# Transfers that take time by size in a planned schedule, merged first loads, copies moved to ScalarE, and later weights converted two at a time

## The chip, the cores and the metric

The kernel runs on one core of a Trainium2 chip. The metric is the device time of one execution in microseconds. Of the kernel before there are three timed executions and one that was profiled. Engines are named as in the profile: PE is TensorE (PEld its weight loads), DVE is VectorE, ACT is ScalarE, POOL is GpSimd, SP issues most transfers.

## The reference

Block-causal attention in float32 over 8 batches and 8 heads, 576 positions of 64 dimensions, and then a feed-forward layer on the 4608 tokens with a parametric ReLU:

```python
scores = (1 / sqrt(64)) * q @ k.T            # 8 x 8 x 576 x 576
mask = (pos[:, None] // 64) >= (pos[None, :] // 64)
attn = softmax(where(mask, scores, -1e9))    # sum + 1e-9 in the divisor
x = (attn @ v)                               # to (4608, 512)
h = x @ w_in                                 # 512 -> 2048
g = maximum(h, 0) + alpha * minimum(h, 0)
out = g @ w_out                              # 2048 -> 512
```

Two of the inputs, w_in and w_out, arrive as float64 (the kernel gets them as pairs of int32) and are turned into float32 on the chip.

## The kernel before

The whole program is a list of operations made by `op(engine, cost, fn, reads, writes, prio, ...)`. `Plan.schedule` (line 121) plays them through once with the costs given and fixes the order in which each engine gets its instructions; at each step an engine takes the ready operation of the lowest `prio` for which buffers are free. On the chip each engine then runs its instructions in exactly that order, and waits where an operand is not there yet. A transfer costs its queue a fixed time (450 to 3300 ns by place) and is over a fixed `LAT` later, whatever its size.

*Attention* runs over 32 pairs of heads, four pairs to a batch. `query_tile` computes a tile of 128 queries: scores on PE, row maximum on DVE (L786, L792), exponential on ACT (L795), sum and reciprocal on DVE (L799, L801), scaling on POOL (L803), transposes on PE (L812) and a copy to SBUF by `evac` (L889 on DVE, L891 on ACT in the first five pairs, NV = 5, which use plain float32). `values` multiplies by v. The first four pairs have their first 256 queries done ahead, from loads of their own (`early`, `load_q`), and pair 0 is done wholly in this way (`rest`). Later pairs are laid out by `prep`, with ten transfers from SBUF to SBUF per pair (L680).

*Weights* are converted by `to_f32` (L396): one transfer of 512 KB, four to five steps on DVE (L411, L416, L420, L425, L428), two on ACT (L414, L423), with two PSUM banks per conversion in flight. `split` (L431) then makes a high part on ACT and a low part on POOL. Six of sixteen slices f of the hidden layer are converted at the start (`first_weights`); the other ten after the attention (`later_weights`), in pairs, each as the factors of a seven-product scheme (`pair1`, L590), with priorities 1000 + f for w_in and 0.5 more for w_out.

*First phase* of the feed-forward layer (`chunk_a`, L512 and L549): 256 tokens at a time through the first six slices, filled in between the attention's work; partial sums go to memory. *Second phase*: 512 tokens at a time (`factors` loads xb and makes seven factors of x; L590 makes hidden parts, L549 multiplies by w_out into one accumulator for each 128 tokens), the other ten slices, and `store_out` adds the partial sums.

PSUM's eight banks are shared out by quotas: six for attention, one for hidden parts (`hp`), one accumulator (`acc`); when the attention ends, two for `hp`, four for `acc` and two for conversions (`words`, one conversion at a time). Some buffers of the second phase, four of the seven factors of x among them, exist only when the first phase has ended (`second_room`). When the last weight is converted, its two banks go to `hp`.

## Time and profile before

| | us |
|---|---|
| median of 3 runs | 1171.3 (1171.28 to 1174.82) |
| profiled execution | 1172.41 |
| its span, first to last instruction | 1170.6 |
| mean granted clock of TensorE | 0.99 |
| busy: PE, DVE, ACT, POOL | 1130.8, 846.4, 724.3, 598.6 |

The span is what the rows below are measured in; the profiled execution's own time lies 1.8 us above it. The engines' busy times add up to far more than the span, as they work side by side. A busy TensorE is not always a TensorE at full pace: products are pipelined, and one that waits for an operand or a bank can count as busy.

### The profile page before, as it was taken

Reading aid. Unit: us, or ns where it says so; the run is one execution under the profiler, and the core shown is the slowest. Engines: PE = TensorE matmul, PEld = TensorE weight load, DVE = VectorE, ACT = ScalarE, POOL = GpSimd, SP = SyncE. Lnnn points to the kernel's source line nnn. Section 1 sums busy time; section 2 is a strip of 40 time slices with the busy share of each in tenths; the row PEclk is TensorE's granted clock in tenths of the full one; section 3 lists DMA queues with packets and bytes.
Section 4 is the critical chain, followed back from the end, with each engine's and each line's share of the span. In section 5 each row is a group of like instructions: output and inputs, shape, how many; then the busy total and the mean of one; then the engine's idle time right before and its main releaser. Section 6 shows DMA issues by size and latency. Waiting matters only on the chain.

```text
span 1170.6 us, 22141 instructions
## 1 busy us (share of the span) xinstructions
PE 1130.8 (97%) x7345; PEld 1010.0 (86%) x7345; DVE 846.4 (72%) x1988; ACT 724.3 (62%) x1940; POOL 598.6 (51%) x771
## 2 busy tenths in 40 slices
PE   6999999999999999999999998999999999999997
PEld 3666899999999999899998986889989898989996
DVE  6988888888887877787867899756556564656543
ACT  5777888878778878687864766543434343343431
POOL 3655555656655556555445978642424344352431
PEclk8999999999999999999999999999999999999999
DMA  7897767776757666647404543302121121212021
GB/s 196 229 251 220 183 181 179 202 199 164 188 138 194 173 166 194 176 111 206 130 19 158 154 152 100 101 19 98 36 73 55 55 73 36 98 38 82 1 73 54
DMA packets 74098, 150.94 MB, mean 129 GB/s; under 512 B 9728, under 2 KB 11520, under 8 KB 73984
## 3 DMA queue, kind: packets, MB, share of 16 engines
q1 hardware_dynamic: 73120, 148.48, 45.2%
q8 instruction: 58, 0.95, 0.4%
q10 hardware_dynamic: 864, 1.06, 0.3%
q14 instruction: 56, 0.46, 0.1%
HBM read 66.33 MB, written 28.31 MB: 81 GB/s over the span
## 4 chain that ended last, share of the span: by engine, by line
PE 84%; DMA 5%; DVE 4%; ACT 2%; POOL 2%; issue 1%; SPq 1%; ACTq 0%; POOLq 0%; DVEq 0%
PE bank L549 32%; PE bank L590 18%; PE bank L512 11%; PE bank L927 6%; PE bank L812 5%; PE bank L779 5%; PE bank L843 2%; PE bank L917 1%; DMA K<-kraw 1%; DMA kraw<-in_k 1%; PE bank L871 1%; DMA Q<-qraw 1%; DMA qraw<-in_q 1%; ACT p L795 1%; SPq L680 1%
## 5 line engine op out<-in xcount | busy, mean ns | idle before, releaser
L532 POOL TENSOR_TENSOR gl<-g,gh 128x256 fp32r<-128x256 f32 x288 | 218.2, 766 | 317.2 <-PE bank L590 150.6
L590 PEld LDWEIGHTS bank<-X,w 128*128 128x128 f32 x1890 | 254.3, 190 | 24.1 <-POOL w L434 3.8
L590 PE MATMUL bank<-X,w 128*128 128x256 f32 x1890 | 260.5, 283 | 4.6 <-POOL w L434 3.4
L549 PE MATMUL bank<-w,gh 128*128 128x512 f32 x720 | 226.4, 395 | 3.0 <-ACT gh L529 2.1
L523 ACT ACTIVATE g<-bank 128x256 f32<-128x256 f32 x288 | 110.4, 385 | 184.5 <-DVE bank L603 164.2
L803 POOL TENSOR_SCALAR p<-p,ri 128x256 f32<-128x256 f32 (+3 forms) x256 | 142.9, 572 | 115.9 <-DVE ri L801 60.6
L529 ACT CAST gh<-g 128x256 fp32r<-128x256 f32 x288 | 117.1, 408 | 73.3 <-DVE g L525 71.8
L525 DVE SCALAR_TENSOR_TENSOR g<-g,oal,bank 128x256 f32<-128x256 f32 x288 | 135.4, 475 | 32.3 <-ACT g L523 28.2
L603 DVE TENSOR_TENSOR bank<-bank,g 128x256 f32<-128x256 f32 x180 | 75.6, 428 | 101.0 <-PE bank L590 78.5
L795 ACT ACTIVATE p<-bank,nm 128x256 f32<-128x256 f32 (+3 forms) x256 | 134.1, 532 | 23.0 <-DVE nm L792 14.3
L549 PE MATMUL bank<-w,gl 128*128 128x512 f32 x360 | 142.0, 395 | 0.3 <-POOL gl L532 0.2
L549 PE MATMUL bank<-wa,gh 128*128 128x512 f32 x432 | 140.6, 406 | 0.3 <-POOL wa L434 0.3
L549 PEld LDWEIGHTS bank<-w,gh 128*128 128x128 f32 x720 | 121.6, 189 | 17.2 <-ACT gh L529 2.5
L512 PE MATMUL bank<-xh,wa 128*128 128x256 f32 x864 | 132.3, 289 | 1.8 <-DVE xh L498 1.0
L894 DVE TENSOR_TENSOR PL<-bank,PH 128x512 fp32r<-128x512 f32 (+2 forms) x189 | 111.6, 608 | 16.8 <-ACT PH L893 13.9
L512 PEld LDWEIGHTS bank<-xh,wa 128*128 128x128 f32 x864 | 115.1, 190 | 5.9 <-DVE xh L498 1.6
L812 PE MATMUL bank<-ident,p 128*128 128x128 f32 x640 | 102.7, 279 | 10.7 <-POOL p L803 7.9
L779 PE MATMUL bank<-K,Q 128*128 128x512 f32 (+1 forms) x472 | 102.0, 333 | 0.9 <-DVE xT L948 0.4
L893 ACT CAST PH<-bank 128x512 fp32r<-128x512 f32 (+2 forms) x189 | 96.4, 529 | 10.5 <-PE bank L812 7.5
L599 DVE TENSOR_TENSOR g<-bank,g 128x256 f32<-128x256 f32 x135 | 57.0, 422 | 56.2 <-PE bank L590 55.1
L812 PEld LDWEIGHTS bank<-ident,p 128*128 128x128 f32 x640 | 73.7, 141 | 20.5 <-POOL p L803 11.7
L927 PE MATMUL bank<-PH,V 128*128 128x320 f32 x324 | 87.6, 286 | 2.0 <-DVE g L525 1.0
(130 smaller groups left out, 2070.7 us busy)
## 6 DMA issues: line engine op xcount, KB each, us to landing
Q<-QH SPq DMA_DIRECT2D x62, 288.0 KB, 4.4
K<-KH SPq DMA_DIRECT2D x124, 144.0 KB, 3.7
vraw<-in_v SPq DMA_DIRECT2D x32, 320.0 KB, 3.3
xd<-xT SPq DMA_DIRECT2D x8, 1152.0 KB, 5.9
part<-o SPq DMA_DIRECT2D x36, 256.0 KB, 3.6
xb<-xd SPq DMA_DIRECT2D x9, 1024.0 KB, 5.4
ob<-part SPq DMA_DIRECT2D x36, 256.0 KB, 2.7
out<-ob SPq DMA_DIRECT2D x36, 256.0 KB, 2.0
```

The costliest lines, as they stand in the source:

```text
L512: nc.tensor.matmul(hp()[:, :n], ww()[:, 0, cc * P:(cc + 1) * P], x()[:, cc, :n], start=(i == 0 and cc == 0), stop=(i == 2 and cc == NCC - 1))
L525: op("DVE", c_dve(CHA) + 60, lambda: nc.vector.scalar_tensor_tensor(out=g(), in0=g(), scalar=oal[:, f:f + 1], in1=hp()[:, ts], op0=ALU.mul ...
L529: op("ACT", c_act(CHA, True), lambda: nc.scalar.copy(out=gh(), in_=g()), r=[g], w=[gh], prio=FP)
L532: op("POOL", c_pool(CHA), lambda: nc.gpsimd.tensor_tensor(out=gl(), in0=g(), in1=gh().bitcast(F32), op=ALU.subtract), r=[g, gh], w=[gl], p ...
L549: nc.tensor.matmul(acc(), a()[:, ts], ww(), start=(first and i == 0), stop=(last and i == 2))
L590: nc.tensor.matmul(bank()[:, :CHA], W()[:, i, 256 * at + P * c:256 * at + P * c + P], B()[:, j, CHA * c:CHA * c + CHA], start=(n == 0), st ...
L779: nc.tensor.matmul(o, Q()[:, i, qs], K()[:, 2 * h + i, :w], start=(i == 0), stop=(i == 1))
L795: op("ACT", 238 + w / 1.2, lambda h=h, t=t: nc.scalar.activation(out=t()[:, :w], in_=sb[h]()[:, off[h]:off[h] + w], func=AF.Exp, bias=nm() ...
L803: op("POOL", 244 + w / 1.2, lambda h=h: nc.gpsimd.tensor_scalar(out=pts[h]()[:, :w], in0=pts[h]()[:, :w], scalar1=ri()[:, h:h + 1], scalar ...
L812: nc.tensor.transpose(out=tp()[:, base + c * P:base + (c + 1) * P], in_=pts[h]()[:, c * P:(c + 1) * P], identity=ident)
L894: op("DVE", c_dve(n) + (HALF if n == P else 0), lambda: nc.vector.tensor_tensor(out=lo(), in0=src(), in1=hi().bitcast(F32), op=ALU.subtrac ...
L927: nc.tensor.matmul(ob()[:, at + a - q0:at + q1 - q0], V()[:, c, 2 * h:2 * h + 2, :], t[:, h, 448 * c + a:448 * c + q1], start=(i == 0 and ...
```

## The change

What it does:

- The planner gives a transfer a time by its size in KB: 430 ns on the queue, 1300 ns to begin, 4.1 ns for each KB on one common pipe, 1000 ns to land, and no more than eight at once (the ninth waits on its queue). All transfers are now given by size.
- The first loads are merged: q of pair 0 in two transfers, q of pairs 1 to 3 in two, k of pairs 1 and 2 in one; they no longer wait for zeros. Zeros of pairs 1 to 3 go to POOL. k of pair 0 stays on ACT's queue; k of pair 3 and the first w_in move from ACT's queue to SP's, the latter with the priority E0 - 6.5. The buffers for these early q and k are others. Fixed parts of Q and K get priority 2 instead of 0.
- In the first five pairs, the second head's copies of tiles 2 and 3 go from DVE to ACT. The first step of a conversion writes the SBUF tile m instead of a PSUM bank, and ACT reads it from there.
- The first two of the later w_in are converted in the attention stage (priority 150, banks of the attention), the others two at a time (four banks for `words`). For that there are two accumulators at first; two banks go over from `words` to `acc` when the w_in of f = 12 is ready. The first xb gets priority 1006.7 instead of 0.

```diff
-BANKS, HB, AB, HT, AT, WB = 6, 1, 1, 2, 4, 2
+BANKS, HB, AB, HT, AM, AT, WB = 6, 1, 1, 2, 2, 4, 4
-XP = 0.0
+XP = 2.0
+SOON, XB = 150, 1006.7
+FEW = 12
-LAT = {"PE": 250, "DVE": 130, "ACT": 140, "POOL": 140, "SP": 3300, "ACTQ": 3000, "POOLQ": 3000}
+LAT = {"PE": 250, "DVE": 130, "ACT": 140, "POOL": 140}
+QUEUES = ("SP", "ACTQ", "POOLQ")
+ISSUE, BEGINS, LANDS, PER_KB, LANES = 430, 1300, 1000, 4.1, 8
...
+                if engine in QUEUES:
+                    begin = max([t, *lands[-LANES:][:len(lands) >= LANES]])
+                    end = begin + ISSUE
+                    pipe = max(begin + BEGINS, pipe) + cost * PER_KB
+                    lands.append(pipe + LANDS)
+                    lat = lands[-1] - end
...
-        op("DVE", c_dve(512), lambda: nc.vector.tensor_scalar(
-            out=e(), in0=high(), scalar1=0x7FF00000, scalar2=None, op0=ALU.bitwise_and),
-            r=[raw], w=[eb], claim=[fb, mb], prio=prio)
-        op("ACT", c_act(512), lambda: nc.scalar.activation(
-            out=e(), in_=e(), func=AF.Relu, bias=ebias, scale=8.0), w=[eb], prio=prio)
+        op("DVE", c_dve2(512), lambda: nc.vector.tensor_scalar(
+            out=mb().bitcast(I32), in0=high(), scalar1=0x7FF00000, scalar2=None, op0=ALU.bitwise_and),
+            r=[raw], w=[mb], claim=[fb, eb], prio=prio)
+        op("ACT", c_act(512, True), lambda: nc.scalar.activation(
+            out=e(), in_=mb().bitcast(I32), func=AF.Relu, bias=ebias, scale=8.0), r=[mb], w=[eb], prio=prio)
...
-                mb, w = to_f32(src[f].bitcast(I32), prio, queue="ACTQ" if f + i == 0 else "SP")
+                mb, w = to_f32(src[f].bitcast(I32), prio, early=E0 - 6.5 if f + i == 0 else None)
...
-            ms = [to_f32(w_in[f + i].bitcast(I32), prio(f), ["att"], "words") for i in range(2)]
+            ms = [to_f32(w_in[f + i].bitcast(I32), *((prio(f), ["att"], "words") if f > FA else (SOON, [], "att"))) for i in range(2)]
...
-        op("SP", 2900, lambda: nc.sync.dma_start(out=xb(), in_=xd[:, :, t0:t0 + CHB]),
-           ... w=[xb], prio=0)
+        op("SP", 1024, lambda: nc.sync.dma_start(out=xb(), in_=xd[:, :, t0:t0 + CHB]),
+           ... w=[xb], prio=0 if t0 else XB)
...
+    def early_loads():
+        def zeros(engine, ps):
+            for h in range(2):
+                rows = slice(64 - 64 * h, 128 - 64 * h)
+                engine.memset(xT[rows, ps, S + 256 * h:S + 256 * h + 256], 0.0)
+        pr = E0 - 8
+        op("DVE", 700, lambda: zeros(nc.vector, slice(0, 1)), w=[("zeros", 0)], prio=pr)
+        op("POOL", 1600, lambda: zeros(nc.gpsimd, slice(1, NP)), w=[("zeros", p) for p in range(1, NP)], prio=pr)
...
+        for p0, p1 in ((0, 1), (1, NP)):
+            for h in range(2):
+                hs = slice(64 * h, 64 * h + 64)
+                op("SP", 64 * (p1 - p0), lambda h=h, hs=hs, p0=p0, p1=p1: nc.sync.dma_start(
+                    out=xT[hs, p0:p1, S + 256 * h:S + 256 * h + 256],
+                    in_=qT[p0:p1, hs, 64 * h:64 * h + 256].rearrange("p r n -> r p n")), w=[("q", p, h) for p in range(p0, p1)], prio=pr)
+        for ps, to, queue in (((0,), lambda: o_k()[:, :256], "ACTQ"), ((1, 2), lambda: o_k2().rearrange("p (i n) -> p i n", i=2), "SP"),
+                              ((3,), lambda: KX[:, :256], "SP")):
+            issuer = {"SP": nc.sync, "ACTQ": nc.scalar}[queue]
+            op(queue, 128 * len(ps), ..., prio=pr + ps[0])
...
-                         p, "DVE" if j == 0 or j > 1 and h else "ACT", pr)
+                         p, "DVE" if j == 0 else "ACT", pr)
...
-        plan.quota["acc"] += AT - AB
+        plan.quota["acc"] += AM - AB
         plan.quota["words"] = WB
...
+    def more_sums():
+        plan.quota["acc"] += AT - AM
+        plan.quota["words"] -= AT - AM
+    op("NONE", 0, lambda: None, r=[(("w1", FEW, 6), "l")], prio=0, then=more_sums)
```

## Rows read from the trace of the kernel before

**Rows 1.** Busy time by stretch: length, then PE, PEld, DVE, ACT, POOL (instructions), clock, DMA share.

```profile
0.00:25.00 25.00, 15.70 (x60) 10.06 (x60) 14.72 (x55) 11.60 (x29) 9.47 (x28) 0.86 0.71 197
25.00:125.00 100.00, 89.68 (x509) 63.91 (x509) 86.47 (x207) 74.05 (x200) 58.47 (x71) 0.98 0.87 229
125.00:600.00 475.00, 471.06 (x3327) 439.25 (x3325) 384.22 (x985) 386.25 (x1101) 263.09 (x369) 1.00 0.64 169
...
633.00:677.00 44.00, 44.00 (x272) 39.38 (x272) 40.13 (x69) 32.05 (x70) 37.69 (x41) 1.00 0.46 139
677.00:740.00 63.00, 55.13 (x313) 46.88 (x313) 58.66 (x113) 41.89 (x93) 51.64 (x53) 0.95 0.33 106
740.00:1150.00 410.00, 410.00 (x2585) 369.99 (x2585) 238.27 (x514) 159.74 (x404) 161.08 (x188) 1.00 0.18 60
```

**Rows 2.** Waits of 0 to 25 us: total, times, longest.

```profile
DVE bank L411 <- DMA raw<-in_w_in: 6.1, 1, 6.1
```

**Rows 3.** Timeline of 0 to 18 us: start, duration, engine and line.

```profile
1.23 0.39 ACTq L731 DMA_DIRECT2D o<-in_k  x1
...
2.11 1.20 SPq L714 DMA_DIRECT2D o<-in_q  x2
...
5.57 0.29 DVE L706 TENSOR_SCALAR o<-o 128x256 f32<-128x256 f32 x1
...
5.92 1.22 PE L774 MATMUL bank<-o,o 128*128 128x256 f32 x2 [2.40 <-DVE o L706]
...
8.00 0.26 PE L775 MATMUL bank<-mask_r,mask_l 128*128 128x64 bf16 x1
...
8.53 0.33 ACTq L409 DMA_DIRECT2D raw<-in_w_in  x1
...
14.10 0.68 DVE L786 TENSOR_REDUCE nm<-bank 128x2 f32<-128x512 f32 x1
...
17.27 0.69 PE L812 MATMUL bank<-ident,p 128*128 128x128 f32 x2 [5.67 <-POOL p L803]
```

**Rows 4.** Chain of work that ended last, 677 to 760 us: start, duration.

```profile
745.40 2.75 PE bank L549 x12
748.15 2.12 PE bank L590 x18
```

**Rows 5.** Busy time of L590 alone, then L549 alone, 677 to 740: PE, PEld.

```profile
677.00:740.00 63.00, 31.49 (x211) 29.32 (x211) 0.95 0.33 106
...
677.00:740.00 63.00, 28.41 (x102) 18.69 (x102) 0.95 0.33 106
```

**Rows 6.** Busy time of a conversion's last step (L428, DVE), in two stretches.

```profile
633.00:677.00 44.00, 6.85 (x10) 1.00 0.46 139
677.00:740.00 63.00, 6.80 (x10) 0.95 0.33 106
```

**Rows 7.** DMA issues: count, KB each, median us to landing.

```profile
xd<-xT SPq DMA_DIRECT2D x8, 1152.0 KB, 5.9
...
raw<-in_w_in SPq DMA_DIRECT2D x15, 512.0 KB, 4.5
...
o<-in_k ACTq DMA_DIRECT2D x1, 128.0 KB, 2.7
```

**Rows 8.** Groups by shape, copies of transposed probabilities: busy us, mean ns.

```profile
L889 DVE COPY PTF<-bank 128x512 f32<-128x512 f32 x10 | 6.8, 685 | 1.7 <-PE bank L812 1.1 <-ACT g L523 0.6
L891 ACT COPY PTF<-bank 128x512 f32<-128x512 f32 x10 | 5.9, 590 | 1.3 <-PE bank L812 1.2
```

**Rows 9.** Lines L411 and L498 (min/median/max ns), and L498's smallest shape (mean).

```profile
L411 DVE TENSOR_SCALAR bank<-raw x32: 680/686/696, 13.5 to 731.2; 128x512 int32<-128x512 int32 x32
...
L498 DVE CAST xh<-xT x48: 221/420/1461, 40.5 to 652.5; 128x512 fp32r<-128x512 f32 x24, 128x128 fp32r<-128x128 f32 x8, 128x384 fp32r<-128x384 f32 x8, 128x256 fp32r<-128x256 f32 x8
...
L498 DVE CAST xh<-xT 128x128 fp32r<-128x128 f32 x8 | 5.2, 671 | 0.0
```

**Rows 10.** Waits of 617 to 634 us: total, times, longest.

```profile
DVE xt L450 <- DMA xb<-xd: 5.3, 1, 5.3
```

More of the change, by code (lines that the diff above doesn't have):

```diff
@@ L132, in schedule @@
         ticks = {0: TICK}
+        lands, pipe = [0.0], 0.0
         def clock(t, c):
@@ L392, in attn_ffn, with to_f32 @@
     op("DVE", 174, lambda: nc.vector.tensor_scalar(out=oal, in0=al, scalar1=-1.0, scalar2=1.0, op0=ALU.mult, op1=ALU.add), w=["oal"], prio=9)
-    def to_f32(src, prio, after=(), use="att", queue="SP"):
+    def to_f32(src, prio, after=(), use="att", early=None):
         raw, eb, fb, mb = Buf("raw"), Buf("bank", use), Buf("bank", use), Buf("m")
@@ L407, in e @@
             return eb().bitcast(I32)
-        issuer = {"SP": nc.sync, "ACTQ": nc.scalar, "POOLQ": nc.gpsimd}[queue]
-        op(queue, 1460, lambda: issuer.dma_start(out=raw(), in_=src), r=after, w=[raw], prio=prio)
-        op("DVE", c_dve(512), lambda: nc.vector.tensor_scalar(
-            out=e(), in0=high(), scalar1=0x7FF00000, scalar2=None, op0=ALU.bitwise_and),
-            r=[raw], w=[eb], claim=[fb, mb], prio=prio)
-        op("ACT", c_act(512), lambda: nc.scalar.activation(
-            out=e(), in_=e(), func=AF.Relu, bias=ebias, scale=8.0), w=[eb], prio=prio)
+        op("SP", 512, lambda: nc.sync.dma_start(out=raw(), in_=src), r=after, w=[raw], prio=prio if early is None else early)
+        op("DVE", c_dve2(512), lambda: nc.vector.tensor_scalar(
[3 more added lines that the diff above has]
+            out=e(), in_=mb().bitcast(I32), func=AF.Relu, bias=ebias, scale=8.0), r=[mb], w=[eb], prio=prio)
         op("DVE", c_dve(512), lambda: nc.vector.scalar_tensor_tensor(
@@ L652, in store @@
         op("ACT", c_act(512), lambda: nc.scalar.copy(out=o(), in_=acc()), r=[acc], w=[o], prio=FP)
-        op("SP", 730, lambda: nc.sync.dma_start(out=to[t:t + P, :], in_=o()), r=[o], w=[(key, t)], prio=FP)
+        op("SP", 256, lambda: nc.sync.dma_start(out=to[t:t + P, :], in_=o()), r=[o], w=[(key, t)], prio=FP)
     def twice(ap):
@@ L677, in prep, with move @@
             out=kraw().bitcast(F32R), in0=kraw(), in1=KH().bitcast(F32), op=ALU.subtract), r=[KH], w=[kraw], prio=pr)
-        def move(to, of, key, src):
-            op("SP", 650, lambda: nc.sync.dma_start(out=to(), in_=of()), r=[src], w=[key], prio=pr)
+        def move(to, of, key, src, kb=144):
+            op("SP", kb, lambda: nc.sync.dma_start(out=to(), in_=of()), r=[src], w=[key], prio=pr)
         qkeys, q2keys, kkeys = [], [], []
@@ L709, in scaled, with tails @@
                w=[key], prio=prio)
-    def load_q(p, q, q0, pr, key):
-        for h in range(2):
-            hs = slice(64 * h, 64 * h + 64)
-            op("SP", 450, lambda h=h, hs=hs: nc.sync.dma_start(out=q()[hs, h], in_=qT[p, hs, q0 + 64 * h:q0 + 64 * h + 256]),
-               r=[("zeros", p)], w=[(*key, h)], prio=pr)
+    def early_loads():
[6 more added lines that the diff above has]
+        op("POOL", 1600, lambda: zeros(nc.gpsimd, slice(1, NP)), w=[("zeros", p) for p in range(1, NP)], prio=pr)
+        def tails():
+            for h in range(2):
+                nc.gpsimd.memset(KX[64 - 64 * h:128 - 64 * h, 256 + 64 * h:320 + 64 * h], 0.0)
+        op("POOL", 400, tails, w=[("zeros", "tail")], prio=pr + 1)
+        for p0, p1 in ((0, 1), (1, NP)):
+            for h in range(2):
+                hs = slice(64 * h, 64 * h + 64)
[5 more added lines that the diff above has]
+            issuer = {"SP": nc.sync, "ACTQ": nc.scalar}[queue]
+            op(queue, 128 * len(ps), lambda ps=ps, to=to, issuer=issuer: issuer.dma_start(
+                out=to(), in_=kT[ps[0]:ps[-1] + 1, :, :256].rearrange("p r n -> r p n") if len(ps) > 1 else kT[ps[0], :, :256]),
+                w=[("k", p) for p in ps], claim=[o_k] if ps == (0,) else [o_k2] if len(ps) > 1 else [], prio=pr + ps[0])
+        for p in range(NP):
+            scaled(p, 256, lambda p=p: plain_k[p]()[:, :256], ("k", p), pr + p)
@@ L731, in early @@
-        op("ACTQ", 450, lambda: nc.scalar.dma_start(out=k()[:, :256], in_=kT[p, :, :256]), w=[("k", p)], claim=held, prio=pr)
-        scaled(p, 256, lambda: k()[:, :256], ("k", p), pr)
-        op("SP", 650, lambda: nc.sync.dma_start(out=vraw()[:, :2], in_=vT[p, :, :2]), w=[(vraw, 0), (vraw, 1)], prio=pr + VE)
+        op("SP", 128, lambda: nc.sync.dma_start(out=vraw()[:, :2], in_=vT[p, :, :2]), w=[(vraw, 0), (vraw, 1)], prio=pr + VE)
         return None, (vraw, [(vraw, 0), (vraw, 1)])
@@ L738, in rest @@
         vraw = Buf("vraw")
[L739 to L743 removed]
+        for h in range(2):
+            hs = slice(64 * h, 64 * h + 64)
+            op("SP", 64, lambda h=h, hs=hs: nc.sync.dma_start(out=xT[hs, 0, S + 256 * h:S + 256 * h + 256], in_=qT[0, hs, 256 + 64 * h:512 + 64 * h]),
+               w=[("q", 0, h)], prio=pr)
+        op("SP", 128, lambda: nc.sync.dma_start(out=o_k()[:, 256:512], in_=kT[0, :, 256:512]), w=[("k", 0, 1)], claim=[o_k], prio=pr)
+        scaled(0, 256, lambda: o_k()[:, 256:512], ("k", 0, 1), pr)
+        op("SP", 32, lambda: nc.sync.dma_start(out=klast(), in_=kT[0, :, 512:S]), w=[("k", 0, 2)], prio=pr)
         scaled(0, 64, klast, ("k", 0, 2), pr)
```

54 lines of the change are left out of this document (19 added, 35 removed).

## The prediction

> **What bounds the kernel now.** I read the busy times by stretch first [rows 1]. TensorE is the bound: from 740 to 1150 it is busy 410 of 410 us, from 125 to 600 it is busy 471.1 of 475. Only time in which it stands, or runs thin, can be won, and the stretches say where that is: in 0 to 25 it is busy 15.7 us at a mean clock of 0.86; in 25 to 125 it stands 10.3 us; in 677 to 740 it stands 7.9 us at clock 0.95. (The end, the last stores, the change leaves alone: same number, same buffers.)
>
> Each place has its own limit, and I went to the waits and the timeline for it. *Front:* VectorE stood 6.1 us for the transfer of the first weight [rows 2], and TensorE 5.67 us for the first scaled probabilities. These are one event: the weight's transfer was issued at 8.53 us on ScalarE's queue, VectorE sat in front of it, the first row maximum came behind it at 14.10, and the first transpose of probabilities could start at 17.27, though the scores were done at 8.26 (the mask product at 8.00 lasts 0.26) [rows 3]. *25 to 125:* VectorE is busy 86.5 of 100 us and the DMA engines 87% [rows 1]; either can be the limit. *677 to 740:* VectorE 58.7 and GpSimd 51.6 of 63 us, both nearly full, while TensorE thins out. In a packed run an L549 product takes 2.75/12 = 0.229 us and an L590 product 2.12/18 = 0.118 us [rows 4]. The 102 and 211 of them in this stretch [rows 5] make 23.4 + 24.9 = 48.3 us of work in 63: 14.7 us are lost, the largest single loss in the kernel. TensorE waits there for the later weights, whose 20 conversions run from 633 to 740, ten in 44 us and ten in 63 [rows 6].
>
> **The change part by part.**
>
> *Front: merged loads, zeros, the first weight on SP.* Now VectorE zeroes all four pairs and builds fixed parts before it may scale the first keys: it gets to that at 5.57, and TensorE starts at 5.92 [rows 3]. With one pair's zeros on VectorE, the rest on GpSimd (which only waits for keys then, and they are done before its first key lands) and the fixed parts at a later priority, the keys' landing sets the start: issued at 1.23 [rows 3], 2.7 us to landing [rows 7] and, because four loads of q go ahead of it, up to 0.8 more; then 0.29 for the scaling and 0.06 to the product. That is 4.3 to 5.1; I take 4.7. The scores last as now, 8.26 - 5.92 = 2.3 us, so the first maximum starts at 7.1. The first weight is issued on SP behind five transfers of some 0.6 us each (two in 1.20 us [rows 3]), near 3.7, and lands 4.5 us later [rows 7], at 8.2: after the maximum, so VectorE no longer stands in front of it. From the maximum to the first transpose it is 17.27 - 14.10 = 3.2 us now, so the transpose starts near 10.4 instead of 17.27: 6.9 us earlier. That is the upper end. What follows is paced by transfers, and the DMA engines idle 29% of the first 25 us [rows 1], 7.2 us, so they can be pulled forward by no more than about as much; the lower end is 0, if the rest of pairs 1 to 3 arrives no sooner. I take 5, because the queue is filled from 0.7 us on and five issues are saved (16 loads of q, k and v become 11).
>
> *25 to 125: ten copies moved.* Two copies of each of five pairs leave VectorE, five of 512 columns at 0.685 us and five of 384: at most 6.9 us, by columns some 6. ScalarE takes them at 0.590 and less [rows 8], some 5.4. VectorE falls from 86.5 to about 80 us in this stretch and ScalarE rises from 74 to 79.5 [rows 1]: even. If VectorE is the limit, up to 6 us come back; if it is the DMA engines, nothing does, as their bytes stay the same. I take 3, the middle.
>
> *The conversion's first step (L411).* It now writes SBUF instead of PSUM. Before: 0.68 to 0.70 us, always. The nearest row is the cast from SBUF to SBUF in L498, whose median is 0.42, but which runs from 0.22 to 1.46 us [rows 9]. So a conversion is between 0.27 us cheaper and 0.77 dearer on VectorE, and GpSimd, which could be what the long ones stood for, is busy 37.7 of 44 and 51.6 of 63 us where the later weights are converted [rows 1]. I take 0.69, no change. ScalarE's step reads SBUF instead of PSUM, some hundredths either way: nothing. The Trainium skill ("SBUF — State Buffer", Who interferes with whom) says that a copy or scalar operation of VectorE from SBUF to SBUF takes a port pair that it shares with GpSimd, and that whichever starts second stands until the first has finished; the spread of L498 agrees, and by that rule this edit speaks against the change.
>
> *Later weights: two begun in the attention stage, four banks, two accumulators at first.* At 617 the attention's buffers come free, and SP issues the spill and xb first. VectorE then stands 5.3 us for xb [rows 10], does the factors, and converts only from 633 on. After the change the first two w_in are converted earlier, in a stretch where VectorE has 384 of 475 us [rows 1], and xb is placed behind the w_out loads of the first pair (1006.7 against 1006.5). Those land with the spill or just after it, 617 + 5.9 us [rows 7], so near 624: 9 us sooner, and 18 conversions remain instead of 20, another 2 x 4.4 = 9 us at the present pace. The factors now fall between conversions: seven operations of 0.69 us [rows 9] or more, some 6 us by estimate. So the twelve conversions that bring the weights up to f = 12 (14 in that order, less two) end near 624 + 12 x 4.4 + 6 = 683, and the last, at 6.3 us each after that, near 720 instead of 740.
>
> What that buys: the first phase's products run out at 677, and the second phase's take 42 x 0.118 + 24 x 0.229 = 10.5 us per pair of f, so TensorE asks for the last w_in at 677 + 42 = 719 and for the last w_out near 724. By then they are there, or nearly. Not won back is what the factors cost: four of seven find a buffer only when the first phase has closed its own, so they are still split after 677; 4 us stay lost there by estimate, and 2 more for weights just in time. 14.7 - 6 = 9 us gain; ends 0 and 13. The two conversions moved into the attention stage cost it ten steps of some 0.69 us on a VectorE that is only 81% busy; I charge 1 us.
>
> *Transfers by size, eight at once.* This is a cost in the planner and adds no instruction. It moves the order on every engine. From 125 to 600 TensorE stands 3.9 us in all [rows 1], so a better order wins at most that; a worse one has no such floor. I take 0, with 3 either way.
>
> **Sum.** -5 - 3 - 9 + 1 = -16 us on the span of 1170.6, so 1154.6. The profiled execution took 1172.4, 1.8 over its span; the median is 1.1 under that. So 1155 on the median.
>
> **The rivals.**
>
> *The front is hidden by the transfers.* If 25 to 125 is bound by the DMA engines, an early start waits for the same bytes: the 5 and the 3 go, 1163. For it: 87% there. Against: 29% idle before.
>
> *The new first step stands behind GpSimd.* L498's smallest shape (128 columns) takes 0.67 in the mean and 0.22 at best [rows 9]. The same 0.45 on 0.42 is 0.87, 0.18 dearer than now, 18 times 3.3 us of an engine that is full from 633 to 740; GpSimd stands too, in its turn. Then the 9 becomes 5: 1159. This is the rule of the Trainium skill named above, carried through.
>
> *More than forecast.* The front keeps its 6.9, the copies give 5 and the transition 13: about 1146. For it: the three stretches lose more than the sum takes.
>
> *Slower: two accumulators.* Until the weights of f = 12 are there, the second phase has two accumulators instead of four. With six buffers each for the hidden parts it can do f = 6 and 8 and most of 10 for half of the tokens, 5.0 + 2.75 + 5.0 + 2.75 + 4.3 + 1.4 = 21 us, and then TensorE stands, from 698 on, one us for each us that the weights are later. I expect them at 683. To lose all of the 16 and 3.5 more they must come at 698 + 20 = 718, that is, conversions of 7 us each instead of 4.4. For it: 63/10 = 6.3 us each after 677 [rows 6]. Then 1175 or more.
>
> **How the numbers follow.** Forecast 0.45, front hidden 0.15, GpSimd 0.13, more 0.15, slower 0.12. A difference under 0.3% (3.5 us) can't be told from none here. A third of the last case and a fifth of the front's land within that: same 0.07, slower 0.08, faster 0.85; I take 0.04 off for an order that goes wrong in a place I can't see: faster 0.81, same 0.08, slower 0.11. Range: from the rival of more, less 2, to the hidden front with 6 us less at the transition: 1144 to 1169.
>
> **What would show it.** First product near 4.7 us, first transpose near 10.4, no long wait of VectorE for a weight in the first 25 us. VectorE and ScalarE near 80 us each in 25 to 125. Six or seven conversions after 677 instead of ten, the last by 725; some 6 us lost from 677 to 740. L411 at 0.42 alone and over 0.8 beside GpSimd. I am wrong if TensorE's idle time at 125 to 600 grows past 8 us, or if it stands at 690 to 720 for accumulators.

## The result, and the profile after

The kernel with the change takes 1165.3 us (median of 8; 1160.95 to 1166.73), the one before, timed beside it, 1173.3: ratio 0.9928, 95% interval 0.9908 to 0.9947, or 8.4 us faster. One of the eight executions of the kernel before took 2825.55 us and is left out of the ratio, which compares the means of the others; the two medians differ by 8.0. The profiled execution took 1165.41 us with a span of 1163.6, 7.0 under the span of before. The forecast was 1155, 16 under the 1171.3 known then: right in direction, inside the range, half of the gain.

Lines have moved in the file: the first weight load is L419, the first step of a conversion L421 (was L411), its last L438 (L428), second phase L601 (L590), products with w_out L560 (L549), first phase L523 (L512), the spill of a batch L981 (L958).

Busy time by stretch after (as in [rows 1]):

```profile
0.00:25.00 25.00, 19.66 (x96) 12.79 (x97) 19.61 (x62) 17.62 (x50) 13.72 (x38) 1.00 0.80 209
25.00:125.00 100.00, 93.20 (x531) 70.15 (x529) 85.14 (x199) 77.87 (x200) 57.43 (x68) 0.97 0.89 238
125.00:600.00 475.00, 468.30 (x3287) 433.52 (x3286) 382.16 (x982) 384.33 (x1099) 263.37 (x368) 1.00 0.64 169
633.00:677.00 44.00, 41.95 (x256) 36.44 (x255) 40.07 (x67) 29.27 (x63) 38.22 (x39) 1.00 0.44 139
677.00:740.00 63.00, 58.51 (x354) 51.11 (x353) 56.34 (x113) 40.26 (x93) 49.68 (x52) 0.97 0.29 96
```

TensorE works 4.0 us more before 25 and 3.5 more from 25 to 125, then 2.8 *less* from 125 to 600 and 2.1 less from 633 to 677, and 3.4 more from 677 to 740. So TensorE leads by 7.5 us at 125, and gives some of that back in two places.

Timeline of the front after (start, duration, engine, line):

```profile
1.20 0.39 ACTq L746 DMA_DIRECT2D o<-in_k  x1
...
3.98 0.46 SPq L419 DMA_DIRECT2D raw<-in_w_in  x1
...
4.85 0.29 DVE L717 TENSOR_SCALAR o<-o 128x256 f32<-128x256 f32 x1
...
5.20 1.22 PE L797 MATMUL bank<-o,xT 128*128 128x256 f32 x2 [1.68 <-DVE o L717]
...
7.58 0.69 DVE L809 TENSOR_REDUCE nm<-bank 128x2 f32<-128x512 f32 x1 [2.26 <-PE bank L798]
...
10.76 0.62 PE L835 MATMUL bank<-ident,p 128*128 128x128 f32 x2
...
11.66 0.42 DVE L421 TENSOR_SCALAR m<-raw 128x512 int32<-128x512 int32 x1
...
18.51 1.40 POOL L687 TENSOR_TENSOR kraw<-kraw,KH 128x576 fp32r<-128x576 f32 x1 [1.55 <-ACT KH L686]
...
18.65 1.55 DVE L421 TENSOR_SCALAR m<-raw 128x512 int32<-128x512 int32 x1
```

First product 5.20 (forecast 4.7), first maximum 7.58 (7.1), first transpose 10.76 (10.4; before 17.27). VectorE comes to the first weight at 11.66, in the middle of other work: the 6.1 us of [rows 2] are gone. The last two lines show the new first step behind a GpSimd operation.

Where the lead goes is seen from the spills, one at the end of each batch of attention. First kernel before, then after (count; shortest, median and longest issue in ns; start of the first and the last):

```profile
L958 SPq DMA_DIRECT2D xd<-xT x8: 567/567/1308, 96.7 to 617.1; - x8
```
```profile
L981 SPq DMA_DIRECT2D xd<-xT x8: 567/570/894, 92.7 to 613.9; - x8
```

The attention ends 3.2 us earlier; from its last spill to the end of the span ("the rest" below) it takes 1170.6 - 617.1 = 553.5 before and 1163.6 - 613.9 = 549.7 after, 3.8 less. The forecast had 7 (-5 - 3 + 1) and 9. Each of these is read from one profiled execution. Three runs below have the attention of this kernel unchanged, in the same order; their last spills come at 610.3, 611.2 and 614.9, so the attention ends 2.2 to 6.8 us earlier than in the one profile of before, 4.5 in the mean of the four. The rest is steadier: it is 548.5 to 550.7 in the eight profiles of the first table below that keep what the change does to the later weights, and 553.5 to 554.2 in the three that have them as before (the kernel before, front alone, copies alone).

### The profile page after: what moved, and what is told of

Read it like the earlier page. It is cut to its first block, busy times and chain, and to the rows that moved or that the text cites. A ratio compares the mean times of both kernels' runs of the same rounds, so it can differ in the third digit from the quotient of the medians.

```text
span 1163.6 us, 22091 instructions
## 1 busy us (share of the span) xinstructions
PE 1130.2 (97%) x7345; PEld 1008.9 (87%) x7345; DVE 841.9 (72%) x1970; ACT 729.3 (63%) x1950; POOL 605.7 (52%) x775
## 4 chain that ended last, share of the span: by engine, by line
PE 81%; DVE 6%; DMA 4%; ACT 3%; POOL 3%; issue 2%; SPq 1%; POOLq 0%; ACTq 0%; DVEq 0%
PE bank L560 31%; PE bank L601 19%; PE bank L523 10%; PE bank L950 6%; PE bank L802 5%; PE bank L835 5%; PE bank L866 2%; PE bank L940 2%; DMA K<-kraw 1%; DMA qraw<-in_q 1%; PE bank L894 1%; POOL p L826 1%; ACT p L818 1%; PE bank L797 1%; DVE V L709 1%
## 5 line engine op out<-in xcount | busy, mean ns | idle before, releaser
L543 POOL TENSOR_TENSOR gl<-g,gh 128x256 fp32r<-128x256 f32 x288 | 221.4, 776 | 320.8 <-ACT gh L540 154.5
L601 PEld LDWEIGHTS bank<-X,w 128*128 128x128 f32 x1890 | 251.7, 189 | 21.8 <-DVE m L438 3.1
L601 PE MATMUL bank<-X,w 128*128 128x256 f32 x1890 | 257.2, 281 | 3.3 <-DVE m L438 2.7
L560 PE MATMUL bank<-w,gh 128*128 128x512 f32 x720 | 225.7, 395 | 0.7 <-ACT gh L540 0.7
L560 PE MATMUL bank<-w,gl 128*128 128x512 f32 x360 | 142.0, 394 | 0.4 <-POOL gl L543 0.4
L560 PE MATMUL bank<-wa,gh 128*128 128x512 f32 x432 | 141.2, 408 | 0.5 <-ACT p L818 0.5
L560 PEld LDWEIGHTS bank<-w,gh 128*128 128x128 f32 x720 | 121.9, 189 | 14.8 <-ACT gh L540 0.9
L523 PE MATMUL bank<-xh,wa 128*128 128x256 f32 x864 | 129.8, 289 | 0.8 <-DVE xT L971 0.7
L523 PEld LDWEIGHTS bank<-xh,wa 128*128 128x128 f32 x864 | 115.9, 191 | 5.5 <-DVE xT L971 1.0
L835 PE MATMUL bank<-ident,p 128*128 128x128 f32 x640 | 105.5, 281 | 6.6 <-POOL p L826 6.2
L560 PE MATMUL bank<-wa,gl 128*128 128x512 f32 x216 | 85.9, 398 | 2.5 <-POOL gl L543 2.5
```

Of the source, the lines that this page charges most:

```text
L523: nc.tensor.matmul(hp()[:, :n], ww()[:, 0, cc * P:(cc + 1) * P], x()[:, cc, :n], start=(i == 0 and cc == 0), stop=(i == 2 and cc == NCC - 1))
L543: op("POOL", c_pool(CHA), lambda: nc.gpsimd.tensor_tensor(out=gl(), in0=g(), in1=gh().bitcast(F32), op=ALU.subtract), r=[g, gh], w=[gl], p ...
L560: nc.tensor.matmul(acc(), a()[:, ts], ww(), start=(first and i == 0), stop=(last and i == 2))
L601: nc.tensor.matmul(bank()[:, :CHA], W()[:, i, 256 * at + P * c:256 * at + P * c + P], B()[:, j, CHA * c:CHA * c + CHA], start=(n == 0), st ...
L835: nc.tensor.transpose(out=tp()[:, base + c * P:base + (c + 1) * P], in_=pts[h]()[:, c * P:(c + 1) * P], identity=ident)
```

## The experiments

All times are medians, the ratios are to the kernel before timed beside each run (its medians lie from 1172 to 1174). The planner deals the order anew for every edit unless I say that it is kept; a control is the change with nothing but the planner's factor on costs altered. The rest and the first and last spill are read from each profile as above.

| run | us | ratio (95%) | first, last spill | rest |
|---|---|---|---|---|
| the change | 1165.3 | 0.9928 (0.9908 to 0.9947) | 92.7, 613.9 | 549.7 |
| front undone | 1169.4 | 0.9968 (0.9956 to 0.9981) | 101.9, 617.8 | 549.8 |
| front alone | 1168.6 | 0.9962 (0.9950 to 0.9974) | 94.2, 611.8 | 553.6 |
| copies undone | 1174.9 | 1.0017 (1.0005 to 1.0030) | 103.5, 624.6 | 549.9 |
| copies undone, factor 1.13 | 1167.1 | 0.9931 (0.9906 to 0.9956) | 91.4, 614.5 | 548.5 |
| copies alone | 1182.0 | 1.0064 (1.0039 to 1.0089) | 104.4, 628.0 | 554.2 |
| first step undone | 1165.4 | 0.9940 (0.9926 to 0.9953) | 93.5, 612.2 | 550.7 |
| no weights in attention | 1167.6 | 0.9955 (0.9939 to 0.9972) | 92.1, 611.1 | 555.7 |
| four sums, one at a time | 1168.8 | 0.9968 (0.9953 to 0.9983) | 90.6, 611.1 | 553.6 |
| old transfer costs | 1167.4 | 0.9953 (0.9935 to 0.9971) | 95.7, 612.2 | 550.5 |
| factor 1.13 (control) | 1167.9 | 0.9958 (0.9943 to 0.9973) | 90.7, 616.5 | 550.6 |
| factor 1.11 (control) | 1162.2 | 0.9893 (0.9866 to 0.9920) | 90.5, 611.0 | 549.0 |

### The front

Undone (all of the early loads, zeros and the place of the first weight as before, new transfer costs kept), and alone (before with the front only):

```diff
-XP = 2.0
+XP = 0.0
...
-                mb, w = to_f32(src[f].bitcast(I32), prio, early=E0 - 6.5 if f + i == 0 else None)
+                mb, w = to_f32(src[f].bitcast(I32), prio, queue="ACTQ" if f + i == 0 else "SP")
...
-    def early_loads():
+    def load_q(p, q, q0, pr, key):
```

> The kernel after the change with the front of before: single early loads that wait for zeros, first weight and three keys on ScalarE's queue, fixed parts at priority 0. Theory (the lead of the front, 7.6 us at the same work at 42 us and 8.9 at 130, is mostly given back by 677, where it is 0.7, because the middle is not paced by TensorE alone): the kernel without it is at most 3 us slower than after, 1163 to 1168. Rival (the front's lead reaches the end, and the middle's loss of 8 us comes from the new order and would be there anyway): 7 to 9 us slower, 1172 to 1175.

> The kernel before the change with the front alone: merged first loads that do not wait for zeros, the first weight on SP, fixed parts at priority 2; everything else, the planner's transfer costs too, as before. Theory (the front brings the attention's end forward by about 4 us and TensorE's further lead is used up where the first phase has no work left): 1167 to 1170, with the last spill near 613 and 553 us from there to the end, as before the change. Rival (without costs by size the first weight is planned too early again, and VectorE stands in front of it): first transpose at 14 us or later and 1170 to 1174.

Undone it costs 4.1 us, alone it gives 4 to 5. Two measurements from opposite ends agree with the 5 of the forecast; each of them has an order of its own, worth some 3 us either way by the controls, and they lie close together. In the first, the outcome falls between the two expected.

### The ten copies

```diff
-                         p, "DVE" if j == 0 else "ACT", pr)
+                         p, "DVE" if j == 0 or j > 1 and h else "ACT", pr)
```

> The kernel after the change with the ten copies of the first five pairs back on VectorE. Theory (the attention's first batches are paced by a chain from engine to engine and not by VectorE's load, so moving 6 us from it to ScalarE brings little): the first batch is spilled within 1.5 us of 92 us and the kernel within 2 us of 1165. Rival (VectorE is the limit in 25 to 125, as the forecast of 3 us took for half true): the first batch is spilled 3 to 6 us later and the kernel is 3 to 5 us slower.

> The ten copies back on VectorE as in the run that took 1174.9, but planned with the factor 1.13, that is, in another order; its partner is the kernel with the change at 1.13 (1167.9, first batch over at 90.7). Theory: the 9.6 us that the copies cost at 1.12 were mostly that order's bad luck: here the first batch is over at 91 to 96 and the time is 1166 to 1172. Rival: the copies on VectorE cost it by themselves, whatever the order: first batch near 101, time 1176 or more.

The third run has the opposite edit, made in the kernel before:

> The kernel before with this one part of the change alone: the ten copies on ScalarE. Before: first batch over at 96.7, time 1173. If the copies are worth the 3 us that were forecast: first batch at 93 to 94, time 1170. Rival, copies worth 10 us by themselves: first batch at 87 to 90, time 1163 to 1165. Rival, the DMA engines bind this stretch and the copies alone give nothing: 96 to 97.5, time 1172 to 1174.

Undone they cost 9.6 us; undone under another order nothing (1167.1 against the control's 1167.9); done alone they make the kernel 7.6 *slower*. Neither expectation of the first run came, and none of the third's. The same ten copies have both signs, so what these runs measure is mostly the order that came with them, and what the copies are worth by themselves is not shown. Where time goes is visible in the kernel with the copies alone, first in its busy times, then in the waits of SP's queue from 45 to 80 us (total, times, longest), then in that queue's timeline:

```profile
50.00:75.00 25.00, 20.38 (x103) 13.37 (x101) 18.54 (x42) 16.44 (x42) 13.16 (x17) 0.93 0.64 179
```
```profile
SPq L409 <- DVE m L425: 10.6, 2, 7.3
```
```profile
49.52 0.33 SPq L666 DMA_DIRECT2D kraw<-in_k  x1
57.25 0.33 SPq L409 DMA_DIRECT2D raw<-in_w_in  x1
60.51 0.33 SPq L667 DMA_DIRECT2D vraw<-in_v  x1
...
62.81 0.62 SPq L680 DMA_DIRECT2D Q<-QH  x1
```

The kernel before in the same stretch, and SP's first Q of the next pair there:

```profile
50.00:75.00 25.00, 21.95 (x127) 15.99 (x126) 20.83 (x45) 18.21 (x45) 13.79 (x16) 1.00 0.96 251
```
```profile
51.13 1.29 SPq L680 DMA_DIRECT2D Q<-QH  x2
```

From 49.85 to 57.25 SP stands in front of a weight load, because a conversion (L425) has not yet released the buffer; v and the next pair's Q and K queue behind it (Q is issued at 62.81, not at 51.13), the DMA share is 0.64 where it was 0.96, all engines do less, and the first batch ends 7.7 us late. The kernel with the copies undone has a wait of this kind (SP for that step, L435 there, 7.2 us in three pieces before 110 us, the longest 3.3); the kernel with the change has 1.0, the one with the copies undone and factor 1.13, which lost nothing, 3.7 in four pieces. That this wait causes the 7.6 and the 9.6 is argued from the traces; no run took it away alone.

### The conversion's first step

```diff
-        op("DVE", c_dve2(512), lambda: nc.vector.tensor_scalar(
-            out=mb().bitcast(I32), in0=high(), scalar1=0x7FF00000, ...
+        op("DVE", c_dve(512), lambda: nc.vector.tensor_scalar(
+            out=e(), in0=high(), scalar1=0x7FF00000, ...
```

> The kernel after the change, with the conversion's first step writing a PSUM bank again, as before the change. Theory (the SBUF-to-SBUF step waits for GpSimd, and VectorE, behind its plan in 617 to 700, makes TensorE stand there): the step is 0.69 us each time instead of 0.42 to 1.55, TensorE loses 2 to 4 us less from 675 to 700, and the kernel is 2 to 4 us faster than after the change, 1161 to 1163. Rival (the step's mean is 0.71 us in the kernel after, as much as before, and the loss has another cause): within 2 us of 1165.

No difference. The step after (min, median, max in ns), and its mean by shape:

```profile
L421 DVE TENSOR_SCALAR m<-raw x32: 406/481/1560, 11.7 to 719.7; 128x512 int32<-128x512 int32 x32
```
```profile
L421 DVE TENSOR_SCALAR m<-raw 128x512 int32<-128x512 int32 x32 | 22.7, 710 | 4.4 <-POOL xl L511 2.5 <-DMA raw<-in_w_out 1.3 <-POOL w L444 0.6
```

Undisturbed it is 0.41 us and no longer 0.68; at 18.65 in the timeline it took 1.55, having begun 0.14 after a 1.40 us operation of GpSimd and ended 0.29 after it. The Trainium skill ("SBUF — State Buffer", Who interferes with whom) has a rule for the operations of VectorE that use the port pair shared with GpSimd, to which copies, casts and scalar operations in a two-port mode belong: the second to start stands until the first is done. That pair of rows agrees. Over 32 conversions the two cancel: the mean is 0.71, where it was 0.69 [rows 9].

### The later weights: what each edit is worth

No weights in the attention stage:

```diff
-... *((prio(f), ["att"], "words") if f > FA else (SOON, [], "att"))) for i in range(2)]
+... prio(f), ["att"], "words") for i in range(2)]
```

> The kernel after the change, but the first two of the later w_in are converted when the attention has ended, like the others. Theory (they run at 97 and 110 us in the trace, not near 580, and take VectorE's time where it is full, but give the transition 9 us of lead): 25 to 125 is 1 to 3 us shorter, the transition 5 to 9 us longer, 1169 to 1172 in all. Rival (the transition does not hang on the weights any more but on the factors of x and the order): the time stays or falls, 1162 to 1166.

Four sums at once, conversions one at a time:

```diff
-BANKS, HB, AB, HT, AM, AT, WB = 6, 1, 1, 2, 2, 4, 4
+BANKS, HB, AB, HT, AM, AT, WB = 6, 1, 1, 2, 4, 4, 2
```

> The kernel after the change, with four accumulators and one conversion at a time from the end of the attention, as before the change. Theory (two conversions at a time are worth little, since VectorE is full from 630 to 740 either way, and two accumulators hold TensorE up at 677 to 698): TensorE loses 3 to 5 us less there, 1160 to 1163. Rival (without two at a time each conversion again waits for ScalarE in between): the last conversion ends 5 to 10 us later and the kernel is 3 to 6 us slower, 1168 to 1172.

The rest grows by 6.0 and 3.9 us, more than the 2.2 by which it varies among the orders above: both parts earn something, and two accumulators cost less than two conversions at a time give (the second edit takes back both). The times show less, 2.3 and 3.4 us; in both profiles the last spill came 2.8 us earlier than in that of the change.

### The later weights: which engine is the limit

Two runs move work from GpSimd to VectorE: the low parts of the ten w_out, and, with them, four sums of each pair.

```diff
-                split(w, hi, lo, 512, [mb], ..., [W], "POOL", prio(f) + .5)
+                split(w, hi, lo, 512, [mb], ..., [W], "DVE", prio(f) + .5)
```
```diff
-            add("POOL", 256, s1, q21, q22, ALU.add, pr, [m1, "att"])
+            add("DVE", 256, s1, q21, q22, ALU.add, pr, [m1, "att"])
```

> The kernel after the change with the low parts of the ten later w_out computed by VectorE instead of GpSimd, planned anew. Theory (after the attention GpSimd sets the pace: 20 us less for it took 4.5 us off what follows the last spill, 24 us less for VectorE nothing): 13 us less for GpSimd bring 2 to 3 us, 1162 to 1163, and the time from the last spill to the end falls from 549.7 to about 547. Rival (VectorE's spare time there is not free, since an operation with two inputs in SBUF stands behind GpSimd, 1.1 us instead of 0.68): the time stays or grows by 1 to 3 us.

> As the kernel with the low parts of the later w_out on VectorE, and the four sums per pair of w_in on VectorE as well: 28 us less for GpSimd from 617 to 726, at least 15 us more for VectorE. Theory (GpSimd sets the pace, VectorE has some 24 us to spare): 3 to 5 us faster than after the change, 1160 to 1162. Rival (VectorE becomes the limit when it gets all of it): slower than the kernel with the low parts alone, 1164 to 1168.

1168.6 and 1170.4, 3.3 and 5.1 us slower than the change; the rest is 554.8 and 555.9, longer by 5 and 6. Three runs keep the order of the change and leave work out. VectorE: the sign and the multiplication by the exponent in the 18 later conversions. GpSimd: low parts of the later weights, set to 0 instead of computed. Then both.

```diff
...
-        op("DVE", c_dve(512), lambda: nc.vector.tensor_tensor(out=mb(), in0=mb(), in1=eb(), op=ALU.mult), ...
+        op("DVE", c_dve(512), lambda: use == "words" or nc.vector.tensor_tensor(out=mb(), ...
```
```diff
+        late = claim and claim[0].kind in ("w1", "w2")
-        op(on, ..., lambda: (nc.gpsimd if on == "POOL" else nc.vector).tensor_tensor(
+        op(on, ..., lambda: nc.gpsimd.memset(lo().bitcast(F32), 0.0) if late else (...).tensor_tensor(
```

> The kernel after the change, in the same planned order, but the 18 conversions after the attention leave out two of VectorE's five steps (the sign and the multiplication by the power of two, so these weights are mantissas alone): 24 us less for VectorE in 617 to 726. Theory (what is left of the transition's loss, some 11 us from 630 to 700, hangs on VectorE, which is full): conversions end 12 to 20 us earlier, the loss falls to under 5 us, 1157 to 1160. Rival 1 (GpSimd is the limit there): a loss of 8 us and more stays, 1163 to 1166. Rival 2 (the buffers of the factors and the order are): the same.

> The kernel after the change, in the same planned order, but GpSimd fills the low parts of the later weights with zeros instead of computing them (the low parts are left out of the products' values): some 20 us less for GpSimd in 617 to 726, and no reading of SBUF by it there. Theory (VectorE is the limit; it only gains what it stood behind GpSimd): the loss in 630 to 700 falls by 2 to 4 us, 1161 to 1164. Rival 1 (GpSimd is the limit): the loss falls by 6 to 9, 1156 to 1159. Rival 2 (buffers and order): within 2 us of 1165.

> After the change, in the same planned order, with both reliefs at once: the later conversions leave out their sign and exponent-multiply steps (about 24 us less VectorE) and the low parts of the later weights are set to 0 instead of computed (about 20 us less GpSimd). From the last spill to the end the kernel with the change takes 549.7 us, with GpSimd relieved 545.2, with VectorE relieved 549.8. Theory: the two engines are the limit of the transition together, so that relief of one only moves the wait to the other: the rest becomes 541 or less, the time about 1155. Rival: what is left after GpSimd's relief are factors that wait for buffers of the second phase, which no relief shortens: the rest stays at 545 and the time at 1158 to 1160. Second rival: ScalarE or the transfers set the pace: 545 too, with ScalarE as the releaser in the waits of 640 to 700.

| run | us | ratio (95%) | last spill | rest |
|---|---|---|---|---|
| less VectorE | 1162.2 | 0.9905 (0.9880 to 0.9930) | 610.3 | 549.8 |
| less GpSimd | 1158.8 | 0.9882 (0.9856 to 0.9909) | 611.2 | 545.2 |
| less of both | 1159.4 | 0.9869 (0.9842 to 0.9896) | 614.9 | 545.2 |

Busy time from 633 on, in the order of the table:

```profile
633.00:677.00 44.00, 41.72 (x263) 36.80 (x261) 33.48 (x49) 30.90 (x68) 37.81 (x39) 1.00 0.52 156
677.00:740.00 63.00, 59.43 (x359) 51.97 (x360) 48.99 (x99) 37.15 (x87) 48.33 (x50) 0.97 0.29 95
```
```profile
633.00:677.00 44.00, 43.47 (x272) 38.25 (x271) 39.46 (x70) 32.51 (x70) 31.04 (x40) 1.00 0.50 156
677.00:740.00 63.00, 60.36 (x382) 53.09 (x381) 57.55 (x117) 37.48 (x86) 36.51 (x50) 1.00 0.31 101
```
```profile
633.00:677.00 44.00, 42.99 (x265) 37.98 (x263) 31.48 (x51) 30.68 (x67) 29.52 (x39) 1.00 0.46 142
677.00:740.00 63.00, 60.55 (x372) 52.50 (x373) 49.89 (x101) 39.10 (x91) 39.19 (x51) 1.00 0.33 106
```

VectorE is busy 13.9 us less in the first of these and the rest does not move; GpSimd is busy 20.3 less in the second, VectorE as much as with the change (97.0 against 96.4), and the rest is 4.5 shorter. Relieving VectorE as well adds nothing. So my theory that the two limit each other falls. GpSimd is the engine whose relief pays, and VectorE at its present load is no limit. The granted clock of 677 to 740 was 1.00 in both runs with GpSimd relieved and 0.97 with the change; but it was 1.00 too with the front undone and with factor 1.11, whose rests are 549.8 and 549.0, so the clock does not make the 4.5. Whether it is GpSimd's time, its reads of SBUF or the way from a weight to its first product that is shortened is not told apart: the memset that takes a low part's place is shorter and reads nothing.

Why handing GpSimd's work to VectorE costs 5 and 6 is not shown. VectorE as the new limit is one explanation, but with the low parts of w_out on VectorE the longest waits of TensorE from 633 to 740 still end with GpSimd:

```profile
PE bank L560 <- POOL gl L543: 4.0, 4, 1.9
PE bank L601 <- POOL w L444: 1.6, 1, 1.6
```

Even with both reliefs TensorE loses some 5 us just after the first phase, by the forecast's count of products. Are those the four factors that find their buffers late? They were left out for the first 512 tokens (three factors used seven times, with as many products), once with both reliefs and once without:

```diff
+            if t0 == 0 and len(X) > 2:
+                X[x] = X[XS[len(X) % 3]]
+                continue
```

> Both reliefs (two steps of the later conversions left out, low parts of later weights set to 0), and in addition the first 512 tokens use three factors of x seven times instead of seven: the four factors that can be split only when the first phase has closed its buffers are left out. Products and their number stay. With both reliefs alone TensorE still lost 5.8 us from 675 to 700, the low part of a factor was written on GpSimd until 680.8, and the rest took 545.2 us. Theory, late buffers of the factors: the loss from 675 to 700 falls to 2 or less and the rest to 540 to 542. Rival, the weights are still late: the loss stays at 5 to 6 and the rest at 544 to 546. A new order alone moved the rest by 1 us in the two controls (549.0 and 550.6 against 549.7).

> The change with three factors instead of seven for the first 512 tokens, and no other relief (the four late factors and their splits left out). The kernel with the change loses 8.3 us from 675 to 700 and needs 549.7 us from the last spill. If late factors are a limit of their own: 3 to 4 us less, rest 545 to 547. If the weights' conversions cover them: less than 1 us, rest 549 to 551.

1159.6 (ratio 0.9887, 0.9867 to 0.9907) and 1165.8 (0.9942, 0.9922 to 0.9962), the rest 545.1 and 551.0: nothing gained. With three factors and both reliefs, TensorE waits longest from 677 to 700 for

```profile
PE bank L561 <- ACT gh L541: 1.2, 1, 1.2
PE bank L561 <- POOL gl L544: 0.7, 1, 0.7
```

that is, for its own hidden parts to come back through ScalarE and GpSimd, with no first-phase product left to do meanwhile. But the planner put the factors of the next 512 tokens into the hole, from 672.9 on, so the test is not clean: the last 5 us stay open between that pipeline's start and the factors.

### The planner's costs, and a new order by itself

The kernel with the change, planned with the old fixed costs of transfers; and, as controls, with nothing but the planner's factor on costs changed from 1.12 to 1.13 and 1.11.

```diff
...
-                    begin = max([t, *lands[-LANES:][:len(lands) >= LANES]])
-                    end = begin + ISSUE
...
+                    end = t + OLD[cost]
```
```diff
-LONGER = 1.12
+LONGER = 1.13
```

> The kernel after the change, but planned with the transfer costs of before: fixed times by kind on the queue and 3300 ns after it, no common pipe, no limit of eight. Theory (the sizes put no work anywhere, they only reorder; the front's and the transition's edits carry the gain): within 3 us of 1165. Rival 1 (the costs by size are what keeps VectorE from standing in front of loads at the start): VectorE again stands several us for the first weight, 25 to 125 is longer, 1169 to 1174. Rival 2 (the new costs lose in the middle): 1158 to 1162, with less than 5 us of TensorE's idle time in 125 to 600.

> The kernel after the change with one number of the planner changed that has nothing to do with it: the other engines' costs stretched by 1.13 instead of 1.12. Theory (part of the differences between these kernels is chance: any other number gives another order, with its own stumbles of 1 to 3 us at places like 455 or 540): the time moves by 1 to 4 us either way from 1165, and the losses in 125 to 600 sit elsewhere. Rival (the order is stable and differences of 2 us and more have causes in the edits): within 1.5 us of 1165 and the same places.

> After the change with no edit but the planner's factor on costs in the long stretch, 1.11 for 1.12: no work is added or removed, only the order is dealt out anew. With 1.13 the time was 1167.9 against 1165.3. Theory: a new order by itself costs or gives some 3 us either way, mostly costs: 1163 to 1170, with the spills moved by up to 4 us in both directions. Rival: 1.13 was an exception, and an order without edits stays within 1 us: 1164.5 to 1166.5.

+2.1, +2.6 and -3.1 us. An order dealt anew, with no work added or removed, moves the time by some 3 us either way; the old costs move it by no more than that. 1162.2 with 1.11 is the fastest complete version measured; its interval overlaps with that of the change.

## Why the prediction came out at half

Two terms of the sum failed: the -9 of the later weights, of which 3.8 came, and the -3 of the copies, of which nothing is seen.

**Front: -5, right.** The chain of times held within 0.5 us, and the two runs give 4 to 5. That is as much as the whole attention gained (3.2 in this profile, 4.5 in the mean of four).

**What is won by 125 is won at the end: a step that failed.** The sum carries "-5 - 3" from the first 125 us to the span. By 125, TensorE had indeed done 112.9 us of work against 105.4, 7.5 more, as if the 8 had come. But whose work was it? First phase alone (first L523, then L560, after; TensorE's busy time and count):

```profile
0.00:125.00 125.00, 15.61 (x96) 0.97 0.87 232
...
0.00:125.00 125.00, 10.67 (x36) 0.97 0.87 232
```

The kernel before, the same two groups (L512, L549):

```profile
0.00:125.00 125.00, 13.45 (x84) 0.96 0.84 222
...
0.00:125.00 125.00, 5.71 (x18) 0.96 0.84 222
```

7.1 of the 7.5 us are first-phase products, done early. They are fill, of which a finished batch gives only so much: before 600 the two kernels did 1515 (1011 + 504) and 1506 (1008 + 498) of them, so of a lead of 30 products about 9 are left (some records can be missing), and TensorE stands 2.8 us more from 125 to 600. What counts is the batch, and the first one ended 4.0 us earlier, the last 3.2 (one profile places it to some 2 us only). The kernel with the front alone shows it from the other side: by 125 its TensorE has done 106.9 us, only 1.5 more than before, and yet its last spill comes 5.3 us earlier and it is 4 to 5 us faster.

**Copies: -3, not seen.** VectorE went from 86.5 to 85.1, not 80: it got other work. Whether VectorE or the DMA engines are the limit of this stretch, the question that the forecast split in the middle, did not decide: with the same ten copies moved the time went from -9.6 to +7.6 us by the order. That it does so through SP's queue is what the traces suggest.

**First step: 0, right** (0.71 in the mean; the rival's 0.87 did not come: the 18 later ones took 0.64 in the mean).

**Later weights: -9, mis-sized; the rest shrank by 3.8. This is the larger miss.** VectorE's pace was right: first step at 621.1 (forecast 624), the last conversion ends at 726.8 (near 720). After, L601 and L560 from 677 to 740:

```profile
677.00:740.00 63.00, 33.03 (x237) 0.97 0.29 96
...
677.00:740.00 63.00, 31.58 (x117) 0.97 0.29 96
```

By the forecast's own count 237 x 0.118 + 117 x 0.229 = 54.8 us of work in 63: 8.2 are lost, not the 6 of the forecast, so 6.5 are gained (some records can be missing here too). TensorE's longest wait there, and the new one from 633 to 677:

```profile
PE bank L601 <- DVE m L438: 2.7, 2, 2.4
```
```profile
PE bank L560 <- POOL gl L543: 2.0, 4, 1.0
```

The first is a weight of the second phase, still late. The second is the price that I left out: TensorE stands 2.05 us of 44 where it stood none [rows 1], for the first phase's own low parts (L543), which come late on GpSimd. With GpSimd relieved it stands 0.53 us there (43.47 busy of 44, above), with VectorE relieved 2.28, so the price is GpSimd's. From 600 to 677 GpSimd now has 22.5 us of splits (L444), where it had 17.5 (L434 before); and the longest of the four waits, 1.0 at 646.5, came behind a split that had itself waited for ScalarE's high part:

```profile
644.45 1.30 POOL L444 TENSOR_TENSOR w<-m,w 128x512 fp32r<-128x512 f32 x1 [2.58 <-ACT w L443]
```

So it is GpSimd's place in the fixed order as well as its load. 6.5 less 2.05 is 4.4, against 3.8 measured.

The step that failed is thus the one from a conversion to a weight. The forecast sized the transition by the times at which VectorE's conversions end, and let TensorE have the weight then; but GpSimd has to split it first, and I had named both engines as "nearly full" and then costed VectorE's alone. The run with the low parts of the later weights set to 0 comes nearest to that assumption, and there the rest is 545.2, 8.3 under before: almost the 9. The trace of before already said so. Of the 7.9 us that TensorE stands there from 677 to 740, 4.7 end with a split of GpSimd and 0.3 with a step of a conversion; the largest of these waits, and two pieces of the chain of [rows 4] that I had passed over:

```profile
PE bank L590 <- POOL w L434: 3.4, 2, 3.1
```
```profile
730.06 2.36 POOL w L434 x2
...
734.48 2.39 POOL w L434 x2
```

In another order of the same work another engine can come last: with the front alone the longest of these waits was 2.8 us, for the high part of a split, on ScalarE. What holds TensorE for the 8.2 us that are still lost is shown in part: relieving GpSimd takes 4.5 off the rest, and some 5 stay open.

**Two conversions moved into attention: +1.** The text had them in the stretch of 125 to 600, where VectorE has room; they ran at 97.6 and 110.6, in the crowded stretch:

```profile
97.55 0.42 DVE L421 TENSOR_SCALAR m<-raw 128x512 int32<-128x512 int32 x1
...
110.63 1.36 DVE L421 TENSOR_SCALAR m<-raw 128x512 int32<-128x512 int32 x1
```

Without them the first spill comes at 92.1 instead of 92.7: in the first batch nothing that can be measured. The last came 2.8 us earlier, within what one profile is uncertain by, so the +1 is neither shown nor refuted.

**Order: 0, with 3 either way.** That was the right size for a blind deal, by the two controls, but not for the copies, where it came to 8 to 10; the 2.8 us lost from 125 to 600 would lie within it. The gains of single edits do not add up: undoing them one by one costs 4.1, 9.6, 0.1, 2.3, 3.4 and 2.1 us, 21.6 in all, where the whole change gives 8.4.

## What to carry to other kernels

When an early stage gets faster, ask whose work TensorE does in the time won: fill that is borrowed from later is given back, and only the stage's own end counts. In a kernel whose order is planned, run an edit beside a control that only deals the order anew; here that was 3 us, and one edit, tried in three orders, looked worth 9.6, nothing and -7.6. Follow a late operand to the last engine that makes it before pricing the first: TensorE's waits in the trace of before named GpSimd, and the sum counted VectorE. An engine's busy share does not say that it is the limit: take work away from each of two full engines in turn, with the order kept.

## What the hardware showed that was not expected

The same bitwise operation on 128x512 words takes 0.41 us from SBUF to SBUF and 0.68 from SBUF to PSUM on VectorE, but 1.55 beside a GpSimd operation. In the kernel with the copies alone a transfer that waited 7.3 us for its buffer held back those behind it on SP's queue, and in the 25 us from 50 to 75 the DMA share was 0.64, against 0.96 in the kernel before.
